# Linear attention and two MLPs on one core: a token's own term as values times sums, added by a product with the identity, instead of a filled diagonal

## The chip, the cores and the metric

The kernel runs on one core of one Trainium2 chip. The metric is the device time of one execution in microseconds (us). Five engines take part: TensorE (PE, matrix products; PEld is its weight load), VectorE (DVE), ScalarE (ACT), GpSimd (POOL) and SyncE (SP, which issues the transfers).

## The reference

A decaying linear attention over 4 batches, 8 heads, 768 tokens and head dimension 48, then two MLPs on the 3072 tokens (384 to 2048 to 384).

```python
for t in range(S):
    cur = einsum('bhd,bhe->bhde', u[None] * k[:, :, t], v[:, :, t])
    y[:, :, t] = einsum('bhd,bhde->bhe', r[:, :, t], state + cur)
    state = w[:, :, t, :, None] * state + einsum('bhd,bhe->bhde', k[:, :, t], v[:, :, t])
x = y.transpose(0, 2, 1, 3).reshape(B * S, H * D)
x = elu(x @ moe_w_in) @ moe_w_out
x = silu(x @ moe2_w_in) @ moe2_w_out
```

A token's own term (`cur`) is `v[t]` times a scalar per head: the sum over d of `r[t,d] * u[d] * k[t,d]`.

## The kernel before

The attention is cut into 24 units: unit n is chunk n // 4 (128 tokens) of batch n % 4, all eight heads. A unit goes through these steps: decays by two scans on DVE (L160, L170); `products`, the product `rk` of r and k (DVE L222); `summed`, eight sums per token by a product with `u_ch` (PE L233, into columns 448 to 455 of a PSUM tile `sums`); the scaled `tq` and `tk` (DVE L241, L248); `far`, a sum of squares of the decays (ACT L178; only the accumulated sum is used, its elementwise result is thrown away, into `am`); scores (PE L295); `ktok`, four transposes of `tk` (PE L261, into columns 0 to 447 of the same PSUM tile `sums`), copied to `kt` by ACT (L267); `past` (PE L350) and `outer` (PE L324), which read and update the state; `within` (PE L369), scores times values into `y`; `update` of the state (DVE L334, L336, ACT L338); `split` of `y` into a high and a low part `xh` (ACT L381) and `xl` (DVE L382). All products are of fp32 data; where two parts stand for one number (`wh`, `wl`; `gh`, `gl`; `xh`, `xl`), three products make one.

The score tile `am` holds for each head a 128x128 matrix. ACT first fills it with the identity scaled by the token's sum (`diag`, L201: one instruction per head, after a copy `dg` of the eight sums out of PSUM, L198). Then DVE (L312, a predicated copy through the mask `upper`) writes the scores over the part above the diagonal, so the diagonal keeps the token's own term and the product with the values adds it. That is the way of units 0 to 8 (`n < SUMMED`, 9). The later units make the own term by another way, which the change does not touch.

Units 0 to 3 run in an opening stage of their own (`dense_units`). From 41.9 us on, block 0 of the first MLP begins: its 16 slots f = 0 to 15 carry the rounds of units 4 to 7. A slot stands in this order in the program: nine products of the hidden layer (PE L451), the split of the slot before (ACT `gh` L473, DVE `gl` L474), the first half of the activation (ACT L458, L460), a step of the round, its second half (DVE `g` L467), nine products of the output layer (PE L482), another step of the round. Weight work is spread over the slots too: `wst` is joined by DVE (L422, L424) and scaled by ACT (L413, L415), then split into `wh` (ACT L436) and `wl` (DVE L437). The steps of a round come as t0, t1, t2, t3, t5, t4; a round works on unit n and prepares unit n + 1. Round 4 stands in slots 0 to 2, round 5 in slots 3 to 6, round 6 in slots 7 to 9, round 7 in slots 10 to 13. Each engine runs its instructions in program order; buffers are reused in turn, and a read or a write waits by semaphore for the earlier users of the tile.

Of the kernel before, what the change touches and what calls it, by code (L numbers as in the profile page):

```python
# [7 lines left out]
F32 = mybir.dt.float32  # L8
F32R = mybir.dt.float32r
BF16 = mybir.dt.bfloat16  # L10
# [3 lines left out]
ACTF = mybir.ActivationFunctionType  # L14
ALU = mybir.AluOpType
# [4 lines left out]
BLOCKS = (4, 4, 4, 4, 4, 4)  # L20
FIRST_ROUNDED = sum(BLOCKS[:2]) + 1
SUMMED = FIRST_ROUNDED
KRAT = 1

ALONE = (sum(BLOCKS[:1]), sum(BLOCKS[:2]))
# [9 lines left out]
def kernel(  # L35
# [21 lines left out]
    nc = tc.nc  # L57
    B, H, S, D = r.shape
    NT, DM = out.shape
    DFF = moe_w_out.shape[0]  # L60
    RB = w_ch.shape[2]
    L = 128
    NCH = S // L
    NU = B * NCH
    NP = H // 2
    KT = DM // 128
# [5 lines left out]
    g_p = ctx.enter_context(tc.tile_pool(name="g", bufs=2))  # L72
# [7 lines left out]
    tok_p = attn.enter_context(tc.tile_pool(name="tok", bufs=2))  # L80
    ch_p = attn.enter_context(tc.tile_pool(name="ch", bufs=2))
    one_p = attn.enter_context(tc.tile_pool(name="one", bufs=1))
# [31 lines left out]
    seed_on = seed[:, 0:W1].rearrange("p (j t) -> p j t", j=NP)[:, :, 0:1]  # L114
    seed_back = seed[:, 1:].rearrange("p (j t) -> p j t", j=NP)[:, :, L:]
    both = one_p.tile([RB, 2 * W1], F32, name="both")
    k_decay = both[:, W1:].rearrange("p (j t) -> p j t", j=NP)[:, :, 0:L]
    rounded = {}

    def setup():  # L120

        zeros = g_p.tile([128, 129], F32, tag="g", name="zeros")
        nc.vector.memset(zeros, 0.0)
        nc.scalar.activation(out=zeros[:, 0:1], in_=zeros[:, 0:1], func=ACTF.Exp)
        p = ps_h.tile([128, 512], F32, tag="h", name="warm")
        for _ in range(WARM):
            nc.tensor.matmul(p[:, 0:128], zeros[:, 1:], zeros[:, 1:], start=True, stop=True)
        nc.vector.memset(seed, 0.0)
        nc.gpsimd.memset(sums, 0.0)
        for s in state:  # L130
            nc.gpsimd.memset(s, 0.0)

    HEAD = (slice(0, D), slice(64, 64 + D))
# [18 lines left out]
    def prep_steps(n):  # L152
# [21 lines left out]
        def far():  # L174

            x = both[:, 0:2 * W1 - 1]
            to = st["af"][0:RB, 0 if n < SUMMED else H * D:].bitcast(BF16)[:, 0:2 * W1 - 1]
            nc.scalar.activation(out=to, in_=x, func=ACTF.Square, accum_out=sums[0:RB, n:n + 1])  # L178

        def whole_decay():  # L180
# [2 lines left out]
                nc.scalar.activation(out=gl, in_=st["g4"][:, :, L:], func=ACTF.Copy)  # L183

        def bonus():
            af = st["af"] = ch_p.tile([128, H * L], F32, tag="am", name="am")
            st["a"] = af.rearrange("p (j e t) -> p j e t", j=NP, e=2)
            if n < SUMMED:
                return
            kn = st["kn"] = af[:, 0:H * D]  # L190
            nc.gpsimd.tensor_tensor(out=kn, in0=st["k"], in1=u_sb, op=ALU.mult)
            nc.gpsimd.tensor_tensor(out=kn, in0=kn, in1=st["r"], op=ALU.mult)

        def diag(part=0):
            if n < SUMMED:
                if part == 0:
                    dg = st["dg_sb"] = tok_p.tile([128, H], F32, tag="dg", name="dg")
                    nc.scalar.activation(out=dg, in_=st["dg"], func=ACTF.Copy)  # L198
                dg = st["dg_sb"]
                for h in range(part * 4, part * 4 + 4):  # L200
                    nc.scalar.activation(  # L201
                        out=st["a"][:, h // 2, h % 2, :], in_=ident, func=ACTF.Copy, scale=dg[:, h:h + 1])
                return
            if part:
                return
            dg = tok_p.tile([128, H], F32, tag="dg", name="dg")
            nc.vector.tensor_reduce(
                out=dg, in_=st["kn"].rearrange("p (h d) -> p h d", h=H), axis=mybir.AxisListType.X, op=ALU.add)
            nc.gpsimd.tensor_tensor(
                out=st["a"].rearrange("p j e t -> p (j e) t"),  # L210
                in0=ident.unsqueeze(1).to_broadcast([128, H, L]),
                in1=dg.unsqueeze(2).to_broadcast([128, H, L]), op=ALU.mult)

        def products():
            if n >= SUMMED:
                return
            if n <= BLOCKS[0]:
                rk = g_p.tile([RB, NP, L], F32, tag="gh", name="rk")
            else:
                rk = st["af"][0:RB, 0:NP * L].rearrange("p (j t) -> p j t", j=NP)  # L220
            st["rk"] = rk
            nc.vector.tensor_tensor(out=rk, in0=st["c"][:, 0], in1=st["c"][:, 1], op=ALU.mult)  # L222

        def summed(p=None):
# [19 lines left out]
                    rounding(tq[rows], *(rounded["q" + i][rows, :, e, :] for i in "hl"))  # L244

        def kt():
            tk = st["kd"] = ch_p.tile([RB, NP, L], F32, tag="tk", name="tk")
            nc.vector.tensor_tensor(out=tk, in0=st["c"][:, 1], in1=k_decay, op=ALU.mult)  # L248
            if n >= FIRST_ROUNDED:
                rounding(tk, rounded["kh"], rounded["kl"])  # L250
# [26 lines left out]
    def pe_steps(n, xt, col, free=None):  # L277
# [76 lines left out]
        def within():  # L354
            y = ps["y"]
            vf = st["v"].rearrange("p j c -> p (j c)")
            for step in range(4):
                for base in range(4):


                    todo = []
                    for kt in range(KT):
                        blk = 4 * kt + base
                        j, i = divmod(blk, 3)
                        ha, hb = (64 + D) * j, (64 + D) * j + 64
                        todo += {0: [(blk, 2 * j, ha)], 1: [(blk, 2 * j, ha + 32), (blk, 2 * j + 1, hb - 16)],
                                 2: [(blk, 2 * j + 1, hb + 16)]}[i]
                    blk, h, c = todo[step]
                    nc.tensor.matmul(  # L369
                        y[32 * base:32 * base + 32, blk // 4, :], vf[:, c:c + 32], st["a"][:, h // 2, h % 2, :],  # L370
                        start=not ch and step == 0, stop=step == 3 or todo[step + 1][0] != blk,
                        skip_group_check=True)

        def split():
# [183 lines left out]
    def round_ticks(n):  # L558
        pe, do = round_parts(n)

        def t0():
            pe["scores"](0)
            do("bonus")
            do("products")
            do("scan")
            load_unit(n + 2, "kr")

        def t1():
            pe["scores"](1)
            if n in ALONE:  # L570
                own = prep_steps(n)
                own["ktok"]()
                own["ktok_copy"]()
            do("scan_back")
            do("whole_decay")
            if n + 1 not in ALONE:
                load_unit(n + 3, "w")
            pe["masked"](0)

        def t2():  # L580
            pe["masked"](1)
            do("summed")
            do("far")
            do("q")
            do("diag")

        def t3():
            do("kt")
            if n + 1 not in ALONE:
                load_unit(n + 3, "c")  # L590

        def t4():
            do("diag", 1)
            if n < SUMMED - 1:
                do("ktok")
                do("ktok_copy")

        def t5():

            pe["past"]()  # L600
            pe["outer"]()
            pe["within"]()
            if n >= SUMMED - 1:
                do("ktok")
            pe["update"]()
            pe["split"]()
            if n >= SUMMED - 1:
                do("ktok_copy")
            load_unit(n + 2, "v")


        return [t0, t1, t2, t3, t5, t4]

    def dense_units(mask):
# [19 lines left out]
        for n in range(-1, count):  # L634
# [40 lines left out]
            if more:  # L675
                w_split()
                w_load()
                if n >= 0:
                    w_scale()
                p["ktok_copy"]()  # L680
                p["diag"](0)
                p["diag"](1)
            if n == -1:
                w_start(0)
            if n == KRAT:
# [5 lines left out]
        pe[count - 1]["update"]()  # L691
        after["q"]()
        after["kt"]()
        load_unit(count + 2, "wc")
        after["far"]()
        after["diag"](0)
        return after
    def prep_rest(at, n, p):

        if n == BLOCKS[0]:  # L700
            if at == 1:
                p["diag"](1)
        elif at == 1:
            p["bonus"]()
            p["products"]()
            p["scan"]()
            p["scan_back"]()
            p["whole_decay"]()
            load_unit(n + 2, "w")
        elif at == 2:  # L710
            p["summed"]()
            p["q"]()
            p["kt"]()
            load_unit(n + 2, "c")
            p["far"]()
            p["diag"](0)
            p["diag"](1)

    pend, po = [], {}
    last = None  # L720
# [39 lines left out]
    with tc.manual_schedule():  # L760
# [8 lines left out]
        load_unit(1, "v")  # L769
        stage_open(3)  # L770
        setup()
        first_alone = dense_units(
            lambda: nc.scalar.activation(out=upper, in_=above_sb, func=ACTF.Copy))

        x2t = {}
# [10 lines left out]
        for j, units in enumerate(BLOCKS):  # L786
# [2 lines left out]
            todo, count, at = [], 6 * len(ticks), 0  # L789
            alone = None  # L790
            if ticks and ticks[0] in ALONE:
                alone = prep_steps(ticks[0]) if j else first_alone

            def tick(part):
                nonlocal at
# [226 lines left out]
```

## Time and profile before

| | |
|---|---|
| time, median of 3 runs | 943.85 us (943.28 to 944.08) |
| the profiled execution's own time | 944.12 us |
| its span in the profile | 942.3 us |
| busy share of the span: PE, DVE, ACT, POOL | 97%, 52%, 53%, 14% |
| opening stage, units 0 to 3 | 0 to 41.9 us |
| block 0 with the rounds of units 4 to 7 | 41.9 to about 128 us |

The span is what the trace covers; the execution's time is some 1.8 us longer than its own span. PE is busy for nearly all of it, but the share is a mean over stages: after 128 us PE hardly waits, before that it does.

### The profile page before, as it was taken

How to read it: one execution, taken by the hardware profiler on the slowest of the kernel's cores; microseconds unless marked ns; L12 is line 12 of the kernel's file. 1: busy time of each engine (PE TensorE's matmuls, PEld its weight loads, DVE VectorE, ACT ScalarE, POOL GpSimd, SP SyncE). 2: the span in 40 equal slices, each digit the busy share in tenths (PEclk: the TensorE clock that was granted, in tenths of full speed). 3: DMA queues.
4: the chain of work that ended last, by engine and by line, in shares of the span. 5: the costliest groups of instructions: out<-in, count | busy, mean ns of one | idle time of the engine just before them, and what ended most of it. 6: DMA issues, size and time to landing. Idle time of an engine off the chain costs nothing.

```text
span 942.3 us, 15209 instructions
## 1 busy us (share of the span) xinstructions
PE 917.9 (97%) x6158; PEld 788.9 (84%) x6158; DVE 493.9 (52%) x726; ACT 501.8 (53%) x901; POOL 132.6 (14%) x101
## 2 busy tenths in 40 slices
PE   7898999999999999999999999999999999999996
PEld 7776688888888888888888899989999999999996
DVE  8988887776776767666378862112212222222211
ACT  6897866566565565654488963323323333333332
POOL 0000013343443344452000000000000000000000
PEclk9799999999999999999999999999999999999999
DMA  8565424122322322310345420200200200200001
GB/s 253 156 180 165 150 61 137 58 67 75 110 66 56 93 65 58 97 49 1 101 166 170 153 82 1 67 1 0 68 1 1 68 1 1 67 1 1 34 1 37
DMA packets 32222, 68.69 MB, mean 73 GB/s; under 512 B 3600, under 2 KB 13968, under 8 KB 32144
## 3 DMA queue, kind: packets, MB, share of 16 engines
q1 hardware_dynamic: 32144, 67.64, 23.1%
q8 instruction: 50, 0.82, 0.4%
q14 instruction: 28, 0.23, 0.1%
HBM read 58.19 MB, written 9.44 MB: 72 GB/s over the span
## 4 chain that ended last, share of the span: by engine, by line
PE 82%; DVE 7%; ACT 4%; issue 1%; ACTq 0%; DVEq 0%
PE ph L451 38%; PE po L490 21%; PE po L482 17%; PE sc L303 2%; PE y L369 1%; PE y L350 1%; DVE gl L474 1%; DVE wst L424 1%; DVE wst L422 1%; DVE g L467 1%; ACT wh L436 1%; ACT am L201 1%; DVE wl L437 1%; DVE am L312 1%; PE ktp L261 1%
## 5 line engine op out<-in xcount | busy, mean ns | idle before, releaser
L474 DVE TENSOR_TENSOR gl<-g,gh 128x512 fp32r<-128x512 f32 x192 | 144.0, 750 | 312.9 <-ACT gh L473 312.5
L451 PE MATMUL ph<-xh,wh 128*128 128x512 f32 x576 | 227.9, 396 | 3.4 <-ACT wh L436 3.4
L451 PE MATMUL ph<-xh,wl 128*128 128x512 f32 x576 | 228.2, 396 | 1.7 <-DVE wl L437 1.7
L451 PE MATMUL ph<-xl,wh 128*128 128x512 f32 x576 | 227.3, 395 | 0.0
L473 ACT ACTIVATE gh<-g 128x512 fp32r<-128x512 f32 x192 | 120.9, 630 | 152.0 <-PE po L490 109.3
L451 PEld LDWEIGHTS ph<-xh,wl 128*128 128x128 f32 x576 | 108.8, 189 | 27.0 <-DVE wl L437 3.6
L462 ACT ACTIVATE g<-ph 128x512 f32<-128x512 f32 x96 | 57.3, 596 | 138.4 <-PE ph L451 137.6
L490 PE MATMUL po<-wh,gl 128*128 128x384 f32 x384 | 129.5, 337 | 0.0
L490 PE MATMUL po<-wh,gh 128*128 128x384 f32 x384 | 129.3, 337 | 0.0
L490 PE MATMUL po<-wl,gh 128*128 128x384 f32 x384 | 129.0, 336 | 0.0
L451 PEld LDWEIGHTS ph<-xh,wh 128*128 128x128 f32 x576 | 108.7, 189 | 24.0 <-ACT wh L436 4.2
L451 PEld LDWEIGHTS ph<-xl,wh 128*128 128x128 f32 x576 | 108.9, 189 | 19.4
L482 PE MATMUL po<-gh,wh 128*128 128x512 f32 x288 | 114.0, 396 | 0.0
L482 PE MATMUL po<-gl,wh 128*128 128x512 f32 x288 | 112.3, 390 | 0.0
L482 PE MATMUL po<-gh,wl 128*128 128x512 f32 x288 | 112.2, 390 | 0.0
L458 ACT ACTIVATE g<-ph 128x512 f32<-128x512 f32 x96 | 56.5, 588 | 50.0 <-PE ph L451 49.8
L467 DVE SCALAR_TENSOR_TENSOR g<-g,ph 128x512 f32<-128x512 f32 x96 | 65.3, 681 | 29.9 <-ACT g L460 29.2
L490 PEld LDWEIGHTS po<-wh,gh 128*128 128x128 f32 x384 | 72.2, 188 | 4.3 <-ACT x2s L501 0.2
L490 PEld LDWEIGHTS po<-wl,gh 128*128 128x128 f32 x384 | 72.1, 188 | 4.1
L490 PEld LDWEIGHTS po<-wh,gl 128*128 128x128 f32 x384 | 72.0, 188 | 0.0
L237 POOL TENSOR_TENSOR ql<-tq,qh 64x512 fp32r<-64x512 f32 (+1 forms) x30 | 42.6, 1419 | 170.6 <-ACT qh L236 169.5
L482 PEld LDWEIGHTS po<-gh,wh 128*128 128x128 f32 x288 | 54.1, 188 | 11.6 <-issue 0.8
(95 smaller groups left out, 1081.5 us busy)
## 6 DMA issues: line engine op xcount, KB each, us to landing
wst<-in_moe_w_in_dram SPq DMA_DIRECT2D x32, 384.0 KB, 3.4
wst<-in_moe_w_out_dram SPq DMA_DIRECT2D x32, 384.0 KB, 4.7
in_c<-in_rk_ch_dram SPq DMA_DIRECT2D x24, 448.0 KB, 4.2
in_w<-in_w_ch_dram SPq DMA_DIRECT2D x24, 226.2 KB, 2.7
in_v<-in_v_tok_dram SPq DMA_DIRECT2D x24, 224.0 KB, 3.9
x_d<-x2s SPq DMA_DIRECT2D x18, 256.0 KB, 2.5
xl<-x_d SPq DMA_DIRECT2D x6, 768.0 KB, 5.2
out_dram<-os SPq DMA_DIRECT2D x24, 192.0 KB, 2.0
```

The costliest lines, as they stand in the source:

```text
L201: nc.scalar.activation(out=st["a"][:, h // 2, h % 2, :], in_=ident, func=ACTF.Copy, scale=dg[:, h:h + 1])
L237: nc.gpsimd.tensor_tensor(out=lo, in0=x, in1=hi.bitcast(F32), op=ALU.subtract)
L261: nc.tensor.transpose(p[:, j, :], st["kd"][:, j, :], ident[0:RB, 0:RB])
L303: nc.tensor.matmul(p[:, jj].rearrange("p e t -> p (e t)"), a[:, j, :], b[:, j].rearrange("p e t -> p (e t)"), start=i == 0, stop=i == len( ...
L451: nc.tensor.matmul(ph, lhs, xt[rhs][:, kt, 0:nt], start=n == 0, stop=n == 3 * KT - 1)
L458: nc.scalar.activation(out=g, in_=ph, func=ACTF.Exp)
L462: nc.scalar.activation(out=g, in_=ph, func=ACTF.Silu)
L467: nc.vector.scalar_tensor_tensor(out=g, in0=g, scalar=-1.0, in1=ph, op0=ALU.mult, op1=ALU.max)
L473: nc.scalar.activation(out=gh, in_=g, func=ACTF.Copy)
L474: nc.vector.tensor_tensor(out=gl, in0=g, in1=gh.bitcast(F32), op=ALU.subtract)
L482: nc.tensor.matmul(po[ot][:, 0:nt], lhs, rhs, start=f == 0 and i == 0, stop=f == NF - 1 and i == 2)
L490: nc.tensor.matmul(po[t][:, 0:DM], lhs[:, sl], rhs["o", f], start=f == 0 and i == 0, stop=f == NF - 1 and i == 2)
```

## The change

For units 0 to 8, ACT no longer fills the diagonal. The two score tiles `am0` and `am1` are now fixed and are set to zero once by POOL in `setup`, so that all but the part above the diagonal stays zero. The own term is made as `vs`, values times sums (128 tokens x 384): on ACT for units 0 to 4 (a copy `dg` and eight 128x48 instructions, L210), on DVE for units 5 to 8 (one 128x384 instruction that reads the sums from PSUM, L203). Twelve products with the identity (PE L368) add it to `y` ahead of the sixteen of `within`. `rk` goes into the `tk` tile that `kt` overwrites later; the waste of `far` goes into the tile `in_w` of the unit; the load of `in_w` for unit n + 3 is issued after `far` (step t2) instead of in t1. `diag`, which stood half in t2 and half in t4, stands whole in t4, ahead of `ktok`.

```diff
-        for s in state:
+        for s in (*ams, *state):
             nc.gpsimd.memset(s, 0.0)
...
         def far():
-            to = st["af"][0:RB, 0 if n < SUMMED else H * D:].bitcast(BF16)[:, 0:2 * W1 - 1]
+            to = st["w"].bitcast(BF16)[:, 0:2 * W1 - 1]
...
-            af = st["af"] = ch_p.tile([128, H * L], F32, tag="am", name="am")
+            af = ams[n % 2]
...
-        def diag(part=0):
+        def diag():
             if n < SUMMED:
-                if part == 0:
-                    dg = st["dg_sb"] = tok_p.tile([128, H], F32, tag="dg", name="dg")
-                    nc.scalar.activation(out=dg, in_=st["dg"], func=ACTF.Copy)
-                dg = st["dg_sb"]
-                for h in range(part * 4, part * 4 + 4):
+                vs = st["vs"] = tok_p.tile([128, NP, 2, D], F32, tag="vs", name="vs", bufs=1)
+                v = st["v"]
+                v3 = bass.AP(v.tensor, v.offset, [v.ap[0], (64 + D, NP), (64, 2), (1, D)])
+                if n > BLOCKS[0]:
+                    nc.vector.tensor_tensor(
+                        out=vs, in0=st["dg"].rearrange("p (j e) -> p j e", e=2).unsqueeze(3).to_broadcast([128, NP, 2, D]),
+                        in1=v3, op=ALU.mult)
+                    return
+                dg = tok_p.tile([128, H], F32, tag="dg", name="dg")
+                nc.scalar.activation(out=dg, in_=st["dg"], func=ACTF.Copy)
+                for h in range(H):
                     nc.scalar.activation(
-                        out=st["a"][:, h // 2, h % 2, :], in_=ident, func=ACTF.Copy, scale=dg[:, h:h + 1])
+                        out=vs[:, h // 2, h % 2, :], in_=v3[:, h // 2, h % 2, :], func=ACTF.Copy, scale=dg[:, h:h + 1])
...
         def products():
-            if n <= BLOCKS[0]:
-                rk = g_p.tile([RB, NP, L], F32, tag="gh", name="rk")
-            else:
-                rk = st["af"][0:RB, 0:NP * L].rearrange("p (j t) -> p j t", j=NP)
-            st["rk"] = rk
+            rk = st["rk"] = st["kd"] = ch_p.tile([RB, NP, L], F32, tag="tk", name="tk")
...
         def within():
+            own = "vs" in st
+            if own:
+                vs = st["vs"].rearrange("p j e c -> p (j e c)")
+                for blk in range(KT * 4):
+                    kt, base = divmod(blk, 4)
+                    nc.tensor.matmul(
+                        y[32 * base:32 * base + 32, kt, :], vs[:, 32 * blk:32 * blk + 32], ident,
+                        start=not ch and kt == 0, stop=False, skip_group_check=True)
...
         def t1():
-            if n + 1 not in ALONE:
-                load_unit(n + 3, "w")
             pe["masked"](0)
         def t2():
             do("far")
+            if n + 1 not in ALONE:
+                load_unit(n + 3, "w")
             do("q")
-            do("diag")
+            if n + 1 >= SUMMED:
+                do("diag")
...
         def t4():
-            do("diag", 1)
             if n < SUMMED - 1:
+                do("diag")
                 do("ktok")
                 do("ktok_copy")
```

Three places show how the instructions stand. The first is DVE in slot 2 of block 0, step t4 of round 4, which prepares unit 5; `xl` is the split of unit 4, `wst` and `wl` are weight work, `g` and `gl` are the slot's activation. Before:

```order
L382 TENSOR_TENSOR xl<-y,xh 128x3x128
L422 SCALAR_TENSOR_TENSOR wst<-wst 128x768
L424 SCALAR_TENSOR_TENSOR wst<-wst 128x768
L467 SCALAR_TENSOR_TENSOR g<-g,ph 128x512
L437 TENSOR_TENSOR wl_0_811<-wst,wh_0_810 128x768
L474 TENSOR_TENSOR gl<-g,gh 128x512
```

And now:

```order
L396 TENSOR_TENSOR xl<-y,xh 128x3x128
L436 SCALAR_TENSOR_TENSOR wst<-wst 128x768
L438 SCALAR_TENSOR_TENSOR wst<-wst 128x768
L481 SCALAR_TENSOR_TENSOR g<-g,ph 128x512
L203 TENSOR_TENSOR vs<-sums,in_v 128x384
L451 TENSOR_TENSOR wl_0_861<-wst,wh_0_860 128x768
L488 TENSOR_TENSOR gl<-g,gh 128x512
```

`vs` of unit 5 is new and stands behind `g` of slot 2 and ahead of `wl`. It reads the tile `sums`; the four transposes of `ktok` write other columns of that tile, stand behind `vs` in the program, and now wait by semaphore for it (before, they waited for `tk` and for the copy `dg` on ACT). For unit 6 `vs` stands between `gl` and the next `wst`, for unit 7 again between `g` and `wl`.

The second place is ACT at the same point of the program; `kt` is the copy of unit 5's transposes, `wh` the weight split. Before:

```order
L381 ACTIVATE xh<-y 128x3x128
L413 ACTIVATE wst<-wst 128x768
L415 ACTIVATE wst<-wst 128x768
L201 ACTIVATE am<-ident,dg 128x128 x4
L267 ACTIVATE kt<-sums 128x448
L436 ACTIVATE wh_0_810<-wst 128x768
L473 ACTIVATE gh<-g 128x512
```

And now:

```order
L395 ACTIVATE xh<-y 128x3x128
L427 ACTIVATE wst<-wst 128x768
L429 ACTIVATE wst<-wst 128x768
L273 ACTIVATE kt<-sums 128x448
L450 ACTIVATE wh_0_860<-wst 128x768
L487 ACTIVATE gh<-g 128x512
```

The four fills of the diagonal are gone; the other four of the unit, in t2, are gone as well.

The third place is PE in the opening stage, from the transposes of unit 1 to the first update of the state; `ktp` takes the transposes there, `early` the sums. Before:

```order
L261 MATMUL ktp<-ident,tk 128x112 x4
L369 MATMUL y<-am,in_v 32x128 x16
L233 MATMUL early<-u_ch,rk 128x2 x4
L324 MATMUL upd<-in_v,kt 32x48 x3
L324 MATMUL upd<-in_v,kt 16x48
```

And now:

```order
L267 MATMUL ktp<-ident,tk 128x112 x4
L368 MATMUL y<-ident,vs 32x128 x12
L383 MATMUL y<-am_101,in_v 32x128 x16
L237 MATMUL early<-u_ch,tk 128x2 x4
L330 MATMUL upd<-in_v,kt 32x48 x3
L330 MATMUL upd<-in_v,kt 16x48
```

The twelve products of unit 0 stand ahead of its `within` and ahead of the sums of unit 2, which read `rk` out of the tile that `tk` of unit 2 overwrites next. Each unit of 0 to 8 has such twelve.

## Rows read from the trace of the kernel before

**Rows 1.** By stretch: length; busy PE, PEld, DVE, ACT, POOL (instructions); PEclk; DMA; GB/s.
```profile
0.00:41.90 41.90, 33.08 (x424) 29.21 (x425) 36.73 (x64) 30.41 (x77) 1.74 (x9) 0.80 0.79 228
41.90:128.00 86.10, 78.58 (x688) 60.08 (x687) 73.19 (x107) 73.80 (x140) 0.00 (x0) 0.94 0.48 148
```
**Rows 2.** PE timeline, block 0, waits: start, us, engine, line, out<-in, count [idle before <-releaser].
```profile
49.30 1.05 PE L233 MATMUL sums<-u_ch,am 112*128 112x2 f32 x8 [1.36 <-DVE am L312]
63.91 0.50 PE L451 MATMUL ph<-xh,wh 128*128 128x512 f32 x1 [0.37 <-ACT wh L436]
64.90 0.50 PE L451 MATMUL ph<-xh,wl 128*128 128x512 f32 x1 [0.26 <-DVE wl L437]
...
76.58 0.54 PE L324 MATMUL upd<-in_v,kt 128*32 128x48 f32 x32 [1.05 <-DVE am L312]
84.66 0.50 PE L451 MATMUL ph<-xh,wh 128*128 128x512 f32 x1 [1.91 <-ACT wh L436]
...
99.26 0.50 PE L451 MATMUL ph<-xh,wl 128*128 128x512 f32 x1 [0.90 <-DVE wl L437]
111.76 0.50 PE L451 MATMUL ph<-xh,wh 128*128 128x512 f32 x1 [1.16 <-ACT wh L436]
```
**Rows 3.** PE timeline around the transposes of unit 5.
```profile
55.06 1.05 PE L369 MATMUL y<-am,in_v 128*32 128x128 f32 x32
...
58.22 0.55 PE L261 MATMUL sums<-ident,tk 112*128 112x112 f32 x4
...
74.67 0.86 PE L350 MATMUL y<-tq,state 112*32 112x128 f32 x24
```
**Rows 4.** DVE timeline there.
```profile
62.09 0.68 DVE L467 SCALAR_TENSOR_TENSOR g<-g,ph 128x512 f32<-128x512 f32 x1
63.89 0.96 DVE L437 TENSOR_TENSOR wl<-wst,wh 128x768 fp32r<-128x768 f32 x1 [1.12 <-ACT wh L436]
```
**Rows 5.** ACT timeline there.
```profile
61.35 1.29 ACT L201 ACTIVATE am<-ident,dg 128x128 f32<-128x128 f32 x4
62.52 0.55 ACT L267 ACTIVATE kt<-sums 128x448 f32<-128x448 f32 x1
62.95 0.91 ACT L436 ACTIVATE wh<-wst 128x768 fp32r<-128x768 f32 x1
```
**Rows 6.** PE and DVE timelines around the transposes of unit 6.
```profile
80.11 0.55 PE L261 MATMUL sums<-ident,tk 112*128 112x112 f32 x4
...
85.52 0.68 DVE L474 TENSOR_TENSOR gl<-g,gh 128x512 fp32r<-128x512 f32 x1
```
**Rows 7.** PE and DVE timelines around the transposes of unit 7.
```profile
102.10 1.07 PE L369 MATMUL y<-am,in_v 128*32 128x128 f32 x32
...
105.28 0.55 PE L261 MATMUL sums<-ident,tk 112*128 112x112 f32 x4
...
107.62 0.56 DVE L382 TENSOR_TENSOR xl<-y,xh 128x384 fp32r<-128x384 f32 x1 [1.39 <-ACT xh L381]
...
109.95 0.68 DVE L467 SCALAR_TENSOR_TENSOR g<-g,ph 128x512 f32<-128x512 f32 x1
```
**Rows 8.** PE and DVE timelines of the opening stage, and PE at 176 us.
```profile
11.28 1.05 PE L233 MATMUL early<-u_ch,rk 112*128 112x2 f32 x8 [0.70 <-ACT dg L198]
...
16.07 1.75 PE L369 MATMUL y<-am,in_v 128*32 128x128 f32 x32
17.77 1.05 PE L233 MATMUL early<-u_ch,rk 112*128 112x2 f32 x8
...
18.91 0.69 DVE L248 TENSOR_TENSOR tk<-in_c,both 112x512 f32<-112x512 f32 x1
...
36.11 1.33 DVE L312 COPY_PREDICATED am<-upper,early 128x512 f32<-128x512 int8 x2 [0.54 <-ACT am L201]
...
176.31 0.57 PE L261 MATMUL ktp<-ident,tk 112*128 112x112 f32 x4 [0.95 <-DVE tk L248]
```
**Rows 9.** Busy time of one stretch behind a wait, columns as in Rows 1.
```profile
85.30:88.90 3.60, 3.34 (x10) 2.13 (x9) 3.33 (x5) 3.57 (x9) 0.00 (x0) 0.56 0.59 197
```

More of the change, by code (lines that the diff above doesn't have):

```diff
@@ L116 @@
     both = one_p.tile([RB, 2 * W1], F32, name="both")
+    ams = [one_p.tile([128, H * L], F32, name=f"am{i}") for i in range(2)]
     k_decay = both[:, W1:].rearrange("p (j t) -> p j t", j=NP)[:, :, 0:L]
@@ L192, in bonus @@
             nc.gpsimd.tensor_tensor(out=kn, in0=kn, in1=st["r"], op=ALU.mult)
-        def diag(part=0):
+        def diag():
             if n < SUMMED:
-                if part == 0:
-                    dg = st["dg_sb"] = tok_p.tile([128, H], F32, tag="dg", name="dg")
-                    nc.scalar.activation(out=dg, in_=st["dg"], func=ACTF.Copy)
-                dg = st["dg_sb"]
-                for h in range(part * 4, part * 4 + 4):
+                vs = st["vs"] = tok_p.tile([128, NP, 2, D], F32, tag="vs", name="vs", bufs=1)
[9 more added lines that the diff above has]
+                for h in range(H):
                     nc.scalar.activation(
-                        out=st["a"][:, h // 2, h % 2, :], in_=ident, func=ACTF.Copy, scale=dg[:, h:h + 1])
-                return
-            if part:
+                        out=vs[:, h // 2, h % 2, :], in_=v3[:, h // 2, h % 2, :], func=ACTF.Copy, scale=dg[:, h:h + 1])
                 return
@@ L246, in kt @@
         def kt():
-            tk = st["kd"] = ch_p.tile([RB, NP, L], F32, tag="tk", name="tk")
+            if n >= SUMMED:
+                st["kd"] = ch_p.tile([RB, NP, L], F32, tag="tk", name="tk")
+            tk = st["kd"]
             nc.vector.tensor_tensor(out=tk, in0=st["c"][:, 1], in1=k_decay, op=ALU.mult)
@@ L370, in within @@
                         y[32 * base:32 * base + 32, blk // 4, :], vf[:, c:c + 32], st["a"][:, h // 2, h % 2, :],
-                        start=not ch and step == 0, stop=step == 3 or todo[step + 1][0] != blk,
+                        start=not ch and step == 0 and not own, stop=step == 3 or todo[step + 1][0] != blk,
                         skip_group_check=True)
@@ L680, in dense_units @@
                 p["ktok_copy"]()
-                p["diag"](0)
-                p["diag"](1)
+                p["diag"]()
             if n == -1:
@@ L693, in dense_units @@
         after["kt"]()
+        after["far"]()
         load_unit(count + 2, "wc")
-        after["far"]()
-        after["diag"](0)
-        return after
+        after["diag"]()
     def prep_rest(at, n, p):
[L700 to L703, printed above, removed]
+        if at == 1:
             p["bonus"]()
@@ L708, in prep_rest @@
             p["whole_decay"]()
-            load_unit(n + 2, "w")
         elif at == 2:
@@ L715, in prep_rest @@
             p["far"]()
-            p["diag"](0)
-            p["diag"](1)
+            load_unit(n + 2, "w")
+            p["diag"]()
     pend, po = [], {}
@@ L771 @@
         setup()
-        first_alone = dense_units(
+        dense_units(
             lambda: nc.scalar.activation(out=upper, in_=above_sb, func=ACTF.Copy))
@@ L791 @@
             if ticks and ticks[0] in ALONE:
-                alone = prep_steps(ticks[0]) if j else first_alone
+                alone = prep_steps(ticks[0]) if j else None
             def tick(part):
```

## The prediction

> **What bounds the kernel now.** I read first the busy time by stretch, to see where PE has idle time at all. In the opening stage PE is busy 33.08 of 41.90 us and DVE 36.73; in block 0 with the rounds of units 4 to 7 PE is busy 78.58 of 86.10, and DVE and ACT are almost equally loaded, 73.19 and 73.80 [rows 1]. Over the whole span PE is at 97%. So PE's sum of work is the bound, and some 16 us in the first 128 are the only place where it waits. Second, PE's timeline of block 0, for what it waits for there. Nine waits make the 7.5 us: 1.36 and 1.05 for the masked scores, 0.37, 1.91 and 1.16 for `wh` from ACT, 0.90 and three of 0.26 for `wl` from DVE [rows 2]. The reader is to see that none is a lack of data from memory: DVE and ACT run a little behind PE. Anything put on DVE or ACT ahead of something PE needs is paid there; anything taken off ACT can give back at most these waits. Third, the timelines of the three engines at the places where the change puts a new dependence.
>
> **The added products.** Twelve products of a 128-token identity stand ahead of the sixteen of `within`. Nearest rows: sixteen of the same shape take 1.05 us, so twelve 0.79, and the twelve of `past`, same columns, take 0.86 [rows 3]. I take 0.8 a unit at full clock. Five units (4 to 8) lie where PE is the bound: 4.0 us; those of units 0 to 3 are in the opening stage, treated at the end of this part.
>
> **The new wait.** It decides the sum. For units 5 to 7 `vs` is made on DVE late in the round (step t4) from the PSUM tile `sums`, and the four transposes of `ktok`, which write other columns of that tile, stand behind it and wait for it. Behind the transposes on PE stand the next slot's hidden or output products, that is all of PE's work; behind them on ACT stand `kt`, then `wh`, and behind that `wl` on DVE. `vs` itself has no row. Its nearest is `xl`, 128x384 from PSUM and SBUF on DVE, 0.56 us [rows 7]; I take that, and bound it by 0.5 below (0.68 for 512 columns [rows 4], scaled to 384) and 0.7 above (the 512 columns themselves, 0.69 [rows 8]).
>
> *Why it must wait at all.* In the opening stage the sums of unit 1 (PE) waited 0.70 us for ACT's copy `dg`, which reads other columns of the same tile [rows 8]: two engines on one tile are kept apart here whatever the columns. By the Trainium skill, "PSUM — Partial Sum Buffer", section "PSUM bank collisions raise a hardware error", two engines on one bank and quadrant of PSUM collide even at disjoint columns, so that such accesses have to be ordered; the trace agrees by that 0.70. If only overlapping columns were ordered, the sum would be that of the first rival below.
>
> *Unit 5.* PE came to the transposes at 58.22 [rows 3]. Now it comes later by 0.8 from the opening stage (below) and 0.8 of unit 4's products: 59.8. On DVE `vs` stands behind `g` of slot 2, which ran from 62.09 for 0.68 [rows 4]; DVE's own lateness from the opening I take as nothing, since it waits for `wh` several times before (the 1.12 us in [rows 4] are one such wait). So `vs` ends at 62.77 + 0.56 + 0.1 of hand-over = 63.4, and PE waits 3.6 us where it waited none. PE is then 5.2 late.
>
> *What this does to DVE.* The transposes end at 63.95, `kt` 0.55 later, `wh` 0.91 later [rows 5]; `wl`, which began at 63.89 [rows 4], begins at about 65.35: DVE is 1.45 late. The four fills that ACT loses here (1.29 us [rows 5]) don't help, since ACT's `kt` now waits for the transposes.
>
> *Unit 6.* From there DVE was busy without a gap worth the name until `xl` of unit 5, so 1.45 stays. `vs` of unit 6 stands behind `gl` at 85.52 [rows 6]: 85.52 + 0.68 + 1.45 + 0.56 + 0.1 = 88.3. PE comes to the transposes at 80.11 [rows 6] + 5.2 + 0.8 (unit 5's products) less the waits that now vanish, because PE is later than what it waited for: 0.37 + 0.26 + 1.05 [rows 2]. That is 84.4: a stall of 3.9, and PE is 8.2 late.
>
> *Unit 7.* Between the two transposes 1.91 + 0.26 + 0.90 vanish [rows 2] and 0.8 is added: 5.9 late, at 105.28 + 5.9 = 111.2 [rows 7]. Here DVE depends on PE's lateness: `within` of unit 6 ended at 103.17 [rows 7] and now at about 109.1; `xh` (0.5) and `xl` (0.56) follow, so `xl` begins at about 110.3 instead of 107.62, 2.7 late, and `g` ends at 109.95 + 0.68 + 2.7 = 113.3 [rows 7]. `vs` to 113.9: a stall of 2.7, and PE is 8.6 late.
>
> *After it.* 1.16 + 0.26 vanish [rows 2], 0.8 is added for unit 7: 8.0. Unit 8's 0.8 falls ahead of a gap of 0.95 that PE has at 176 for a DVE result [rows 8]; DVE is not late there, so the gap takes it up. `vs` of unit 8 has PE with other work in front of its transposes; nothing.
>
> **The opening stage.** Unit 0's twelve products run where sixteen took 1.75 us [rows 8], so 1.3 us. They push the sums of unit 2, at 17.77 for 1.05 [rows 8], to an end of 20.1; `tk` of unit 2, at 18.91 on DVE [rows 8], now overwrites what these sums read, and waits until then: 1.2. DVE is the busiest engine of the stage [rows 1], so it carries that on, less the 0.54 that it waited for ACT's fills at 36.11 [rows 8], which are gone: 0.7, and I take 0.8 with PE's own tail. Bounds: nothing (DVE's other gaps take it) and 1.5.
>
> **Edits at nothing.** Clearing the two score tiles is POOL's, busy 1.74 of 41.90 us [rows 1]; if that were late, the first masked scores would wait for it. The load of `in_w` for a unit three rounds on comes one step later; if not hidden, a scan on DVE would wait. ACT loses some 2.6 us of fills a unit (twice 1.29 [rows 5]), which is counted in the waits that vanish.
>
> **Sum.** 0.8 (opening) + 4.0 (products, 4 to 8) + 3.6 + 3.9 + 2.7 (stalls) − 1.68 − 3.07 − 1.42 (waits gone) − 0.8 (gap at 176) = +8.0. On the profiled execution's 944.12 that is 952.1; this execution lies 0.27 above the median of the runs, so 951.9.
>
> **Rivals.**
>
> 1. *The other side: the transposes find `vs` done.* If they need not wait for it, or DVE makes `vs` of unit 5 by 59.8 (it would have to come 3.6 earlier; that is the point from which it decides), there are no stalls, and ACT's relief closes the waits on `wh` and `wl`, 3.44 + 1.68. Then 0.8 + 4.0 − 5.1 − 0.8 = −1.1: 942.7. For it: ACT loses twice 1.29 us a unit [rows 5], which is more than the waits on it. Against it: `g` of slot 2 alone begins at 62.09, and the order puts `vs` behind it. Chance 0.07.
>
> 2. *DVE comes earlier.* `xl` waits 1.39 for ACT's `xh` and `wl` 1.12 for `wh` [rows 7, 4]; if ACT's 2.6 us a unit bring these forward, `vs` of units 6 and 7 is done some 2.5 sooner, and PE's lateness after unit 7, which `vs` sets, falls by as much, to 3.5 with unit 5's share of 2: about +4.5, 948.4. Against it: `xh` waits for DVE and PE, not for ACT's fills, and `kt` waits for `vs`. Chance 0.18.
>
> 3. *The clock falls behind each stall.* Behind the wait of 1.91 the granted clock was 0.56, a mean of the two levels 1.2 and 2.4 GHz, for 3.6 us [rows 9], which costs 0.44 x 3.6 = 1.6. Such a stretch behind unit 5 or 6 is taken up by the next stall, since DVE sets its end; behind unit 7 one takes the place of one already there after the wait at 111.76. If two more count: +3.2, 955.1. Chance 0.10.
>
> **How the numbers follow.** The forecast as summed has 0.65. Its own bounds: the opening stage 0 to 1.5, `vs` ±0.2 at three places, DVE's lateness 0 to 0.8, one stretch at the lower clock more or less (1.6): 949.5 to 954.5. The range reaches into rivals 2 and 3: 947.5 to 955.3, leaving out rival 1 and the far part of rival 2. A measurement of this kernel tells about 0.2% (1.9 us) from no change: faster 0.05 and same 0.06 (both mostly rival 1 and what lies between it and rival 2), slower 0.89.
>
> **What would show it.** Right: PE's `ktok` of units 5, 6, 7 idle for 3.6, 3.9 and 2.7 us, released by DVE `vs`, at about 60, 84 and 111; the waits on `wh` and `wl` in between gone; `y<-ident,vs` at 0.8 a unit; `tk` of unit 2 a little later than 18.91. Wrong: `vs` well before 62 (DVE's order in time differs from what I read), `ktok` released by something else, stalls near nothing with PE's busy time up by 4, or a PE clock below 1 over long stretches after 66.

## The result, and the profile after

The changed kernel takes 953.5 us in the median of 6 runs (951.01 to 955.58); the kernel before takes 943.93 (943.06 to 944.73, 6 runs). The ratio is 1.0101, 95% interval 1.0083 to 1.0118: slower by 1%. The forecast was 951.9 with a range of 947.5 to 955.3. The profiled execution took 952.77, with a span of 950.8, which is 8.5 longer than before.

By stretch (columns as in [rows 1]), the stretch from 41.9 us to the end of block 0 has grown from 86.1 to some 94 us:

```profile
0.00:41.90 41.90, 32.98 (x509) 29.40 (x510) 34.44 (x60) 27.11 (x74) 3.52 (x11) 0.80 0.72 209
41.90:136.00 94.10, 81.33 (x789) 64.51 (x788) 76.65 (x115) 67.99 (x116) 0.00 (x0) 0.93 0.46 143
168.00:950.80 782.80, 776.19 (x4823) 675.14 (x4821) 357.97 (x518) 376.44 (x642) 122.23 (x86) 1.00 0.18 55
```

PE works 81.33 us there instead of 78.58, so under 3 us of the loss is work; the rest is waiting. From 168 us on (last row) PE hardly waits, so the loss lies ahead of that. PE's timeline has just four waits in block 0 where [rows 2] had nine:

```profile
52.09 1.87 PE L237 MATMUL sums<-u_ch,tk 112*128 112x2 f32 x8 [2.93 <-ACT kt L273]
65.84 1.01 PE L267 MATMUL sums<-ident,tk 112*128 112x112 f32 x4 [2.59 <-DVE vs L203]
91.07 0.60 PE L267 MATMUL sums<-ident,tk 112*128 112x112 f32 x4 [3.33 <-DVE vs L203]
115.54 0.60 PE L267 MATMUL sums<-ident,tk 112*128 112x112 f32 x4 [3.93 <-DVE vs L203]
```

The last three are the transposes of units 5, 6 and 7, released by `vs`: 9.85 us of stall that were not there before ([rows 3, 6, 7] show the same transposes without a wait). All the waits on `wh` and `wl` are gone. The first is where the sums of unit 5 waited 1.36 before [rows 2]; it is longer, and has another releaser. That one was not foreseen, and the other engines' timelines tell where it comes from. DVE, from unit 2's `tk` in the opening stage to `vs` of unit 5:

```profile
21.82 0.69 DVE L254 TENSOR_TENSOR tk<-in_c,both 112x512 f32<-112x512 f32 x1 [2.04 <-PE early L237]
...
46.37 0.69 DVE L226 TENSOR_TENSOR tk<-in_c 112x512 f32<-112x512 f32 x1 [2.28 <-DMA in_c<-in_rk_ch_dram]
...
64.64 0.68 DVE L481 SCALAR_TENSOR_TENSOR g<-g,ph 128x512 f32<-128x512 f32 x1
65.23 0.55 DVE L203 TENSOR_TENSOR vs<-sums,in_v 128x384 f32<-128x384 f32 x1
```

Before, the second of these stood at 42.58, and `kt` of unit 4 on ACT at 48.16:

```profile
42.58 0.69 DVE L222 TENSOR_TENSOR am<-in_c 112x512 f32<-112x512 f32 x1 [0.98 <-DMA in_c<-in_rk_ch_dram]
...
48.16 0.52 ACT L267 ACTIVATE kt<-ktp 128x448 f32<-128x448 f32 x1
```

ACT now, in the first slot and at the transposes of unit 5:

```profile
46.99 1.91 ACT L210 ACTIVATE vs<-in_v,dg 128x48 f32<-128x48 f32 x8 [2.03 <-DMA in_v<-in_v_tok_dram]
...
51.52 0.52 ACT L273 ACTIVATE kt<-ktp 128x448 f32<-128x448 f32 x1
...
66.88 0.54 ACT L273 ACTIVATE kt<-sums 128x448 f32<-128x448 f32 x1 [2.87 <-PE sums L267]
```

And PE in the opening stage, where unit 0's products come:

```profile
17.34 1.51 PE L368 MATMUL y<-ident,vs 128*32 128x128 f32 x24
18.62 1.93 PE L383 MATMUL y<-am,in_v 128*32 128x128 f32 x32
20.49 1.29 PE L237 MATMUL early<-u_ch,tk 112*128 112x2 f32 x8
...
41.31 2.05 PE L647 MATMUL early<-ident 128*128 128x128 f32 x16
43.12 0.48 PE L465 MATMUL ph<-xh,wh 128*128 128x512 f32 x1
...
83.74 0.85 PE L368 MATMUL y<-ident,vs 128*32 128x128 f32 x24
84.39 1.07 PE L383 MATMUL y<-am,in_v 128*32 128x128 f32 x32
```

The end of that stage before, for comparison:

```profile
38.95 3.20 PE L632 MATMUL early<-ident 128*128 128x128 f32 x16
41.91 0.48 PE L451 MATMUL ph<-xh,wh 128*128 128x512 f32 x1
```

Read together: `tk` of unit 2 waits 2.04 us for the sums that still read `rk` in its tile. DVE carries this on; the weight work that frees a staging buffer comes later, the loads that stand behind it on SP's queue are issued later (`in_w` at 38.10 against 34.78), and data for unit 5 (`in_c`, for DVE) and unit 4 (`in_v`, for ACT's `vs`, which the old fill did not need) come 2.28 and 2.03 us after their engine is ready (before, `in_c` came 0.98 late). So ACT's `kt` of unit 4 stands at 51.52 instead of 48.16, and PE's sums of unit 5 wait for it.

The loss can be added up on PE. The first hidden product starts 1.2 later (43.12 against 41.91). The stage's own work ends 2.4 later (41.31 against 38.95); the products `early<-ident` behind it, which feed nothing, pass in 1.81 us instead of 2.96, because the granted clock there is 1.00 instead of 0.59, and so hide the other half. The wait at the sums of unit 5 grows by 2.93 − 1.36 = 1.57, the stalls add 9.85, the eight other waits of block 0 (6.17) are gone, the products move what follows by 0.65 in each of units 4 to 8 (83.74 to 84.39 in the rows above), 3.25, and the gap of 0.95 at 176 us [rows 8] is closed: 1.2 + 1.57 + 9.85 − 6.17 + 3.25 − 0.95 = 8.75, against 8.5 measured.

This sum leaves out the clock inside block 0, and closes only because that nearly cancels. From the sums of unit 5 to the first output product PE now takes 8.81 us at a granted clock of 0.63, where it took 6.73 at 0.75 (before, then now):

```profile
49.30:56.03 6.73, 6.73 (x105) 5.36 (x105) 5.80 (x8) 6.67 (x15) 0.00 (x0) 0.75 0.56 163
52.09:60.90 8.81, 8.81 (x130) 7.24 (x130) 8.74 (x14) 7.76 (x13) 0.00 (x0) 0.63 0.65 196
```

With the waits and products taken off, PE loses 1.6 us in this way ahead of the transposes of unit 5 and 1.0 ahead of those of unit 6, and gains 2.2 ahead of those of unit 7, where the stretch of [rows 9] no longer comes, and 0.7 behind them. None of this moves the end of a stall, since `vs` on DVE sets it: time that PE loses ahead of a stall makes the stall shorter.

### The profile page after: what moved, and what is told of

The parts are those of the page before. It is cut to its first block, busy times and chain, and to the rows that moved or that the text cites. A ratio compares the mean times of both kernels' runs of the same rounds, so it can differ in the third digit from the quotient of the medians.

```text
span 950.8 us, 15623 instructions
## 1 busy us (share of the span) xinstructions
PE 922.5 (97%) x6374; PEld 795.2 (84%) x6374; DVE 494.7 (52%) x730; ACT 490.9 (52%) x865; POOL 134.5 (14%) x103
## 4 chain that ended last, share of the span: by engine, by line
PE 90%; DVE 5%; ACT 1%; issue 1%; DMA 1%; SPq 0%; ACTq 0%; DVEq 0%
PE ph L465 40%; PE po L504 21%; PE po L496 19%; PE sc L309 2%; PE y L383 2%; PE y L356 2%; DVE wst L438 1%; DVE wst L436 1%; DMA in_v<-in_v_tok_dram 1%; PE ktp L267 1%; DVE wl L451 1%; PE upd L330 1%; DVE am L318 1%; DVE gl L488 0%; PE y L368 0%
## 5 line engine op out<-in xcount | busy, mean ns | idle before, releaser
L465 PEld LDWEIGHTS ph<-xh,wh 128*128 128x128 f32 x576 | 109.1, 189 | 20.5 <-issue 0.8
```

Source lines behind the costliest of these rows:

```text
L465: nc.tensor.matmul(ph, lhs, xt[rhs][:, kt, 0:nt], start=n == 0, stop=n == 3 * KT - 1)
```

## The experiments

Theory 1: the transposes' wait for `vs` is the loss. Theory 2: the late opening stage and its late loads set the loss, and the stalls only show where it is paid. Unless said otherwise a time is a median, and a ratio is to the kernel before on the same chip. Each diff is against the kernel named.

**1. The sums copied early** (against the changed kernel).

```diff
+        def sums_copy():
+            if BLOCKS[0] < n < SUMMED:
+                dg = st["dg_sb"] = tok_p.tile([128, H], F32, tag="dg", name="dg")
+                nc.scalar.activation(out=dg, in_=st["dg"], func=ACTF.Copy)
...
-                        out=vs, in0=st["dg"].rearrange("p (j e) -> p j e", e=2).unsqueeze(3).to_broadcast([128, NP, 2, D]),
+                        out=vs, in0=st["dg_sb"].rearrange("p (j e) -> p j e", e=2).unsqueeze(3).to_broadcast([128, NP, 2, D]),
...
         def t2():
+            do("sums_copy")
```

> The changed kernel, but for units 5 to 8 ACT copies the eight sums out of PSUM in step t2 (128x8, as before the change), and vs on DVE reads that copy, so the transposes no longer wait for vs. Theory 1 (the wait of the transposes for vs, 9.85 us in the profile, is what costs): the three stalls at ktok vanish, PE's old waits for wh and wl come back in part, and the time falls by most of the loss, to 944 to 947. Theory 2 (the late opening stage, +2.8 us on PE at the sums of unit 5, and the load that comes late there, set the loss, the stalls only show it): PE waits at other places by as much, and the time stays at 950 or more.

943.04 us, ratio 0.9987 (0.9977 to 0.9996). The whole loss is gone and a little more, although the opening stage is nearly as late as in the changed kernel (the sums of unit 5 at 51.57 for 52.09): PE's timeline of block 0 now has

```profile
51.57 1.87 PE L242 MATMUL sums<-u_ch,tk 112*128 112x2 f32 x8 [3.04 <-ACT kt L278]
85.97 0.50 PE L470 MATMUL ph<-xh,wh 128*128 128x512 f32 x1 [0.51 <-ACT wh L455]
86.96 0.51 PE L470 MATMUL ph<-xh,wl 128*128 128x512 f32 x1 [0.26 <-DVE wl L456]
99.78 0.50 PE L470 MATMUL ph<-xh,wl 128*128 128x512 f32 x1 [1.66 <-DVE wl L456]
```

The wait of 3.04 stays and is made good later, because waits of [rows 2] shrink or go. Theory 2 expected 950 or more; it falls as an account of the whole. The time is also just below the lower end that theory 1 gave (944).

**2. `rk` in a tile of its own for units 0 to 4** (against the changed kernel).

```diff
+            if n <= BLOCKS[0]:
+                rk = st["rk"] = g_p.tile([RB, NP, L], F32, tag="gh", name="rk")
+            else:
                 rk = st["rk"] = st["kd"] = ch_p.tile([RB, NP, L], F32, tag="tk", name="tk")
...
-            if n >= SUMMED:
+            if n >= SUMMED or n <= BLOCKS[0]:
                 st["kd"] = ch_p.tile([RB, NP, L], F32, tag="tk", name="tk")
```

> The changed kernel, but rk of units 0 to 4 has a tile of its own as before the change, so that tk of a unit does not wait for the sums that read rk. Theory 1: the 2.04 us that DVE waits at tk of unit 2 vanish, the opening stage is 1 to 2 us shorter at the sums of unit 5, and the whole gains about as much, 1 to 2 us, to about 951.5 to 952.5, with the three stalls at ktok still there. Theory 2: the gain is 5 us or more, to 948 or less.

950.0 us, ratio 1.0056 (1.0039 to 1.0073). DVE's `tk` of unit 2 waits for nothing; the sums of unit 5 and the three transposes all come 2.2 us earlier, with the same stalls:

```profile
49.83 1.87 PE L240 MATMUL sums<-u_ch,tk 112*128 112x2 f32 x8 [2.58 <-ACT kt L276]
63.65 1.01 PE L270 MATMUL sums<-ident,tk 112*128 112x112 f32 x4 [2.50 <-DVE vs L203]
88.88 0.60 PE L270 MATMUL sums<-ident,tk 112*128 112x112 f32 x4 [3.24 <-DVE vs L203]
113.32 0.60 PE L270 MATMUL sums<-ident,tk 112*128 112x112 f32 x4 [3.94 <-DVE vs L203]
```

The median gives 3.5, the two profiles' spans 1.6 (950.8 and 949.2); the executions of the changed kernel lie 4.6 us apart, so the size is known to within some 2 us. Theory 1 expected 1 to 2, theory 2 5 or more; the median lies between them. Either way it is the smaller part. The stalls keep their size because PE and DVE's `vs` come earlier by the same amount.

**3. Only the late read, in the kernel before.**

```diff
+        def late():
+            if BLOCKS[0] < n < SUMMED - 1:
+                vs = tok_p.tile([128, NP, 2, D], F32, tag="vs", name="vs", bufs=1)
...
+                nc.vector.tensor_tensor(
+                    out=vs, in0=st["dg"].rearrange("p (j e) -> p j e", e=2).unsqueeze(3).to_broadcast([128, NP, 2, D]),
+                    in1=v3, op=ALU.mult)
         def t4():
             do("diag", 1)
             if n < SUMMED - 1:
+                do("late")
                 do("ktok")
```

> The kernel before with one thing added: for units 5 to 7 DVE makes vs from the PSUM sums at the place where the changed kernel has it, its result unused, so that only the wait of the transposes (and 0.56 us of DVE a unit) is new. Theory 1: three stalls of PE at ktok of 4.5, 4 and 3 us, the old waits on wh and wl gone, +5 to +7 us: 949 to 951. Theory 2: the stalls are small without the late opening, under +3: below 947.

953.93 us, ratio 1.0106 (1.0084 to 1.0128): this one wait, with nothing else of the change, costs what the whole change costs (10.0 us against 9.6). So the rest of the change comes to about nothing, as experiment 1 says too. PE's waits at the transposes:

```profile
63.73 0.98 PE L270 MATMUL sums<-ident,tk 112*128 112x112 f32 x4 [6.55 <-DVE vs L219]
90.85 1.01 PE L270 MATMUL sums<-ident,tk 112*128 112x112 f32 x4 [4.53 <-DVE vs L219]
117.65 0.98 PE L270 MATMUL sums<-ident,tk 112*128 112x112 f32 x4 [4.13 <-DVE vs L219]
```

15.2 us of stall in place of the waits of [rows 2], of which 1.24 at the sums of unit 5 stay. Theory 1 has its direction right, its size was 949 to 951. The first stall is 6.55, not 4.5: `vs` ends at 63.6, close to the 63.4 of the prediction, but PE comes to the transposes at 57.2.

**4. Only the products, in the kernel before.**

```diff
+            own = n < SUMMED
+            if own:
+                for blk in range(KT * 4):
+                    kt, base = divmod(blk, 4)
+                    nc.tensor.matmul(
+                        y[32 * base:32 * base + 32, kt, :], none, ident,
+                        start=not ch and kt == 0, stop=False, skip_group_check=True)
```

> The kernel before with twelve products of a zero tile with the identity added ahead of within in units 0 to 8, 0.65 to 0.85 us of PE each, nothing else changed (they add zero to y). If the products cost what they take in block 0, five times 0.65 = +3.3 and the opening stage up to +1: 947 to 948. If the waits that PE has there (7.5 us) take them up, under +2: below 946.

944.53 us, ratio 1.0006 (0.9996 to 1.0016): 108 added products (48 in the opening stage, 48 in block 0, 12 in unit 8) cost nothing that can be told here. The first hidden product even starts 1.1 earlier, at 40.85 instead of 41.91, because the products `early<-ident` ahead of it ran at a granted clock of 1.00 and not 0.59. The sums of unit 5 wait for DVE all the same and start at 49.75 instead of 49.30. PE's waits of block 0 fall from 7.5 to 7.0:

```profile
39.04 2.05 PE L641 MATMUL early<-ident 128*128 128x128 f32 x16
40.85 0.47 PE L460 MATMUL ph<-xh,wh 128*128 128x512 f32 x1
...
49.75 1.43 PE L235 MATMUL sums<-u_ch,am 112*128 112x2 f32 x8 [2.88 <-DVE am L314]
84.70 0.50 PE L460 MATMUL ph<-xh,wh 128*128 128x512 f32 x1 [0.89 <-ACT wh L445]
85.69 0.50 PE L460 MATMUL ph<-xh,wl 128*128 128x512 f32 x1 [0.26 <-DVE wl L446]
96.60 0.50 PE L460 MATMUL ph<-xh,wh 128*128 128x512 f32 x1 [0.24 <-ACT wh L445]
99.29 0.50 PE L460 MATMUL ph<-xh,wl 128*128 128x512 f32 x1 [1.96 <-DVE wl L446]
111.78 0.50 PE L460 MATMUL ph<-xh,wh 128*128 128x512 f32 x1 [0.48 <-ACT wh L445]
112.77 0.51 PE L460 MATMUL ph<-xh,wl 128*128 128x512 f32 x1 [0.26 <-DVE wl L446]
```

The starts behind the waits on `wh` and `wl` are those of [rows 2] within 0.04 us (84.70, 99.29 and 111.78 for 84.66, 99.26 and 111.76): ACT and DVE set them, and PE's added work fits into the time ahead of them. Of the gap of 0.95 at 176 us, 0.30 is left.

**5. The own term behind the transposes** (against experiment 2).

```diff
         def t4():
             if n < SUMMED - 1:
-                do("diag")
                 do("ktok")
                 do("ktok_copy")
+                do("diag")
```

> The second experiment (rk of units 0 to 4 in its own tile) with one thing more: in step t4 the own term stands in the program behind ktok and its copy, not ahead of them. On each engine the order of the instructions stays the same; only the waits turn round: the transposes wait for tk alone, and vs on DVE waits for ACT's copy kt. Theory 1 (the wait of the transposes is the loss): 950.0 falls by 7 us or more, to 943 or less. Theory 2 (something else that comes with vs on DVE or with the twelve products): it stays above 948.

941.46 us, ratio 0.9973 (0.9963 to 0.9983); experiment 2 had 950.0 (on another chip, where the kernel before took 943.92 against 944.12 here). No instruction is added, removed or moved on any engine; three waits are turned round, and 8.5 us go. DVE's `vs` of units 5 to 7 now waits once, for 0.53:

```profile
63.63 0.55 DVE L203 TENSOR_TENSOR vs<-sums,in_v 128x384 f32<-128x384 f32 x1
87.03 0.56 DVE L203 TENSOR_TENSOR vs<-sums,in_v 128x384 f32<-128x384 f32 x1 [0.53 <-ACT kt L276]
110.67 0.55 DVE L203 TENSOR_TENSOR vs<-sums,in_v 128x384 f32<-128x384 f32 x1
```

This is the cleanest of the runs: `vs` on DVE, its place there and the products are all as in experiment 2, so none of them is the loss by itself.

**6. Experiments 1 and 2 together.**

> The first and the second experiment together: vs of units 5 to 8 from ACT's early copy of the sums, and rk of units 0 to 4 in its own tile. If the late opening of the first experiment is still paid, it falls by the 2 to 3.5 us that the second gave, to 940 to 941. If the waits that PE then has again on wh and wl take it up (PE runs ahead of DVE once more), it stays near 942 to 943.

941.55 us, ratio 0.9977 (0.9967 to 0.9987): between the two cases. The gain on experiment 1 is 1.5 in the medians and 2.0 in the profiles' spans. PE's waits on `wh` and `wl` do not take the earlier opening up: they are 0.37, 0.26 and 1.67, where experiment 1 had 0.51, 0.26 and 1.66, and stand 1.84 earlier.

**7. The load of `u_sb` later** (against experiment 6).

```diff
-KRAT = 1
+KRAT = 3
```

> The kernel with both, and the load of u_sb (1.09 us on the queue, 192 KB, ahead of in_w and in_c of unit 5 and in_v of unit 4) issued behind the loads of the opening stage. If the late loads hold DVE and ACT at the start of block 0 (waits of 2.0 and 1.6 us there), those come about 1 us earlier and the time falls by up to 1 us against the kernel with both; if the loads wait for their buffers and for weights that land at the same time, nothing changes.

940.56 us, ratio 0.9958 (0.9942 to 0.9975), the fastest of the kernels that add the own term. DVE no longer waits for `in_c`, and the sums of unit 5 begin at 48.91 instead of 49.66. The gain of 1.0 on experiment 6 is as expected, but the intervals overlap, so it is not shown.

**8. Experiment 6 without the products.**

```diff
-                for blk in range(KT * 4):
+                for blk in ():
                     kt, base = divmod(blk, 4)
...
-            own = "vs" in st
+            own = False
```

> The kernel with both, without the twelve products (the own term is left out of y; vs is still computed on ACT for units 0 to 4 and on DVE for 5 to 8). If the products are paid on PE: five times 0.65 = 3.3 us less than the kernel with both. If the waits of block 0 take them up: under 1.5 less.

939.97 us, ratio 0.9956 (0.9940 to 0.9973), 1.6 less than with them: about half of what they take on PE in units 4 to 8 (3.25), and just past the 1.5 that the second answer allowed. PE's waits grow again (2.91 at the sums of unit 5, 1.68 on `wh`, 1.68 on `wl`).

**9. Unit 4's own term later** (against experiment 7): the copy of its sums stays, `vs` on ACT stands behind the first slot's activation.

```diff
-        after["diag"]()
+        after["sums_copy"]()
...
+        if n == BLOCKS[0]:
+            if at == 2:
+                p["diag"]()
-        if at == 1:
+        elif at == 1:
```

> The kernel with both and the later u_sb load, and ACT's vs of unit 4 moved behind the first slot's activation (the copy of its sums stays where it was), so that ACT no longer holds that activation while in_v of unit 4 is on its way. If this hold is what makes kt of unit 4, and with it the sums of unit 5, late on PE (1.2 us left), the time falls by up to 1 us below 940.6; if ACT's work is only moved, it stays within 0.5 us.

941.21 us, ratio 0.9965 (0.9953 to 0.9977): no gain. Against the kernel before on its own chip it is 3.3 us less, where experiment 7 is 3.6 less.

**10. Experiment 5 with the later `u_sb`.**

> The kernel with the own term behind ktok (no copy of the sums) and the later u_sb load. If the later load is worth what it was with the copies (1 us), 940.5; the extra copies of the sums on ACT should make no difference, so within 0.5 us of the kernel with copies and the later load.

940.91 us, ratio 0.9970 (0.9958 to 0.9981): within 0.5 of experiment 7, so the copies of the sums on ACT make no difference that this can tell. Against experiment 5 the gain is 0.55, which this can't tell from none either.

**11. The later `u_sb` in the kernel before.**

> The kernel before with the later u_sb load alone. If the gain of that load belongs to the opening stage in any case (a wait of 0.98 us for in_c was there before too), about 943; if it came only with the changed order of loads, 944.

944.58 us, ratio 1.0001 (0.9992 to 1.0010): nothing. DVE's wait for `in_c` falls only from 0.98 to 0.78, and the sums of unit 5 start at 49.38 instead of 49.30, so in the kernel before this load is not what keeps PE waiting there.

## Why the prediction was right

The direction, the mechanism and its three places were as forecast, and the time lies in the range; the likeliest time was 1.6 short in the medians, and 0.65 by the profiled executions (952.77 for 952.1). Part of that closeness is luck: PE and DVE were both later than worked out, and a stall is the difference of the two. By its own steps:

- *The transposes wait for `vs`.* Right, and shown alone: experiment 3 makes the loss from it, experiments 1 and 5 take it away. The prediction's reason, that the order is kept whatever the columns, is what the program does here; whether it has to was not tried. Releaser and places were as written; the stalls measured 2.59, 3.33 and 3.93 for 3.6, 3.9 and 2.7, together 9.85 for 10.2. At unit 5 PE came 3.5 later than thought (63.25 for 59.8) and `vs` 2.4 later; at unit 6 PE 3.3 and `vs` 2.7; at unit 7 PE 0.4 and `vs` 1.6.
- *DVE's lateness*, taken as nothing up to unit 5, 1.45 behind it and 2.7 at unit 7: mis-sized, and it is what sets PE's lateness. DVE's `g` ahead of unit 5's `vs` began 2.55 late (64.64 for 62.09 [rows 4]); the stall made that 4.37 (`wl` at 68.26 for 63.89 [rows 4]), and it stayed there: 4.34 at unit 6 (`gl` at 89.86 for 85.52 [rows 6]) and 4.39 at unit 7 (`g` at 114.34 for 109.95 [rows 7]). The step for unit 7 was wrong in its reading too. It let `xl` follow PE's `within` and put it at 110.3, which the 109.1 and 0.5 beside it do not give (109.6). In [rows 7] `xl` began 4.45 after `within` had ended. In both traces it waits 1.39 for `xh`, which stands on ACT behind `state`, and that waits for DVE's own `packed`. So DVE carries its own lateness there, and rival 2, in which it came earlier, went the other way.

```profile
68.26 0.96 DVE L451 TENSOR_TENSOR wl<-wst,wh 128x768 fp32r<-128x768 f32 x1 [2.48 <-ACT wh L450]
...
89.86 0.68 DVE L488 TENSOR_TENSOR gl<-g,gh 128x512 fp32r<-128x512 f32 x1
...
110.71 0.75 ACT L344 ACTIVATE state<-packed 48x192 f32<-48x192 f32 x2 [0.76 <-DVE packed L342]
112.01 0.56 DVE L396 TENSOR_TENSOR xl<-y,xh 128x384 fp32r<-128x384 f32 x1 [1.39 <-ACT xh L395]
...
114.34 0.68 DVE L481 SCALAR_TENSOR_TENSOR g<-g,ph 128x512 f32<-128x512 f32 x1
```

- *`vs` costs what `xl` costs*: 0.55 for 0.56, with 0.06 to the transposes; the 0.1 of hand-over stood on no row.
- *The waits that vanish*: 1.68, 3.07 and 1.42, all gone.
- *Rival 1's price*, 942.7 if the transposes need not wait: experiments 1 and 5 gave 943.04 and 941.46. The sum without the new wait came out as near as the one with it.
- *The products*, 0.8 a unit on PE: 0.85 for the twelve by the row, but what stands behind moves by 0.65, since the next products overlap. Where PE waits anyway they cost less still: nothing that can be told in experiment 4, 1.6 us in all in experiment 8. So the 4.0 of the sum was too much.
- *The opening stage*, 0.8: mis-sized, and the source of DVE's 2.55. It measured 1.2 at the first slot and 2.8 at the sums of unit 5. Two things failed in it. PE was already late when unit 0's products came, because the stretch ahead of them ran at a granted clock of 0.50 (11.74 to 17.34 us), where it was 0.79 before (11.28 to 16.07; the sums of unit 1 took 1.87 instead of 1.05 in [rows 8]), so DVE's `tk` waited 2.04, not 1.2. And "edits at nothing" did not see the loads: they stand on the queue behind weight loads that wait for DVE, and ACT's `vs` of unit 4 needs `in_v`, which the fill never did. Experiment 7's gain, itself not clear of the noise, did not come with the kernel before (experiment 11), which fits; how the 2 us divide between DVE's lateness and the queue was not separated.
- *The lower clock behind stalls* (rival 3) added no length that can be told: behind the transposes of units 5 and 7 the granted clock was 0.64 for some 4 us, and behind unit 6 it was 1.00.

```profile
65.80:70.00 4.20, 4.16 (x15) 3.47 (x16) 1.74 (x3) 1.93 (x4) 0.00 (x0) 0.64 0.05 13
...
91.00:95.00 4.00, 3.93 (x20) 3.32 (x21) 2.76 (x5) 3.29 (x5) 0.00 (x0) 1.00 0.96 321
...
115.50:119.50 4.00, 3.96 (x14) 3.18 (x15) 1.96 (x3) 1.85 (x3) 0.00 (x0) 0.64 0.24 56
```

The first of these stretches is taken up by the next stall, as the prediction had it; the last stands in place of one of the same kind as in [rows 9] that followed the wait at 111.76 [rows 2].

By the Trainium skill, "PSUM — Partial Sum Buffer", section "PSUM bank collisions raise a hardware error", any two engines that touch one bank and quadrant have to be ordered, reads too. The trace agrees as to what is ordered: with the program order turned round in experiment 5, `vs` on DVE waits 0.53 for ACT's copy of other columns of the tile, where both only read. What happens without the wait no run here shows.

By the Trainium skill, "ScalarE: Activation LUTs", section "What ACT_TABLE_LOAD costs", an ACTIVATE takes 186 ns and 0.833 ns for each element, 93 more for a pointer operand, and neighbours overlap by 93. For eight of 128x48 that gives 1.90 us, an estimate; the row has 1.91.

## What to carry to other kernels

When work goes to another engine, look not only at what it costs there but at who must wait until that engine has come to it: three times 0.55 us on DVE cost 10 us on PE, because the reader stood behind other work on DVE and PE's next write into the same PSUM tile stood behind the reader. Which of two uses of a tile comes first in the program can be chosen freely where they don't depend on each other; putting the late reader behind the writer that PE needs, with nothing else changed, turned 950.0 into 941.5. A tile that is shared to save space makes the same kind of wait: `rk` in the `tk` tile cost 1.5 to 3.5 us (experiments 6 and 2).

## What was not expected of the hardware

With the three late reads alone (experiment 3), 15.2 us of stalls stood in place of 6.3 us of waits, and the time rose by 10.0, not 8.9; the mean granted clock of that run's profile was the lowest of all, 0.977 against 0.983 to 0.988, and behind the first two stalls it was 0.50 for 5.9 and 4.7 us. That the clock makes up the rest fits, but was not separated. And added products on PE were nearly free even in block 0, where PE was busy 91% of the time: 108 of them, 48 there, moved the time by 0.6 us, which is inside the interval. The cause that the rows show is that DVE and ACT set PE's starts there.
